# A written order for Sinkhorn-sorted attention and a gated MLP: whole K copies, an early flag, one more turn by DMA, and two output tiles of their own

## The chip, the cores and the metric

One core of one Trainium2 chip runs the kernel. The core has five instruction queues: PE (TensorE, the matrix products), DVE (VectorE), ACT (ScalarE), POOL (GpSimd) and SP (SyncE, which here only issues DMAs). Each runs its own list of instructions in order and waits on semaphores for the others. Sixteen DMA engines, shared by all queues, move data. The metric is device time in microseconds of one execution; smaller is better.

## The reference

The inputs are q, k and v of 4 batches, 8 heads, 768 positions and 64 dimensions, one 8x8 matrix for each head (`sort_net`), and the weights of the second part.

```python
P = sort_net
for _ in range(5):
    P = P - np.max(P, axis=-1, keepdims=True)
    P = np.exp(P)
    P = P / (np.sum(P, axis=-1, keepdims=True) + 1e-09)
    P = P / (np.sum(P, axis=-2, keepdims=True) + 1e-09)
k_sorted = np.einsum('bhij,bhjcd->bhicd', P, k_b).reshape(B, H, S, D)
v_sorted = np.einsum('bhij,bhjcd->bhicd', P, v_b).reshape(B, H, S, D)
# in each of 8 blocks of 96 positions:
attn = softmax(scale * q_b @ k_sorted^T);  x = attn @ v_sorted     # to (4, 768, 512)
...
h = np.maximum(x @ w_in, 0.0)                                      # 512 -> 1024
u, v = h[..., :512], h[..., 512:]
v_n = (v - mean(v)) / np.sqrt(var(v) + 1e-06)
v_s = np.einsum('ts,bsd->btd', w_spatial, v_n) + b_spatial[None, :, None]
return ((u * v_s) @ w_out).astype(np.float32)
```

So each batch goes through mixing K and V by P, attention in blocks, and a gated MLP whose gate mixes the 768 positions by `w_spatial`.

## The kernel before

The whole program is written out as a list of some 350 short items in the string `ORDER`. Each item names a unit (a function `u_XX`) and its arguments, and a loop at the end calls them in that order; each unit adds its instructions to the queues of the engines that it uses. The order of an engine's queue is therefore the order of the items that use it, across units. There is no scheduler behind it. Waits follow from the data and from the buffers.

An item such as `KT:2:DA:0:1` reads: unit KT, PSUM tile `ps2`, copied out half by DVE and half by ACT, batch 0, pair of heads 1. There are four PSUM tiles (`ps0` to `ps3`), and each unit that takes one waits until the copy of its previous user is done. A copy letter is A (ACT), D (DVE), or two letters, which split the copy into halves, side by side. The units that matter here, with the lines that the profile names:

- `L` (L156): a load issued by POOL, converted to bf16 on the way; q, k and v of a batch, the two halves `wv` and `wu` of `w_in`, the halves `wsa` and `wsb` of `w_spatial`, and `wo`. Loads of q, k, v and w_spatial share eight buffers (`ld`).
- `ID`, `MA`, `MB`, `MC`: the identity matrix and the masks made of it. `SK` (L223): one of five rounds that normalise P (L231 to L244), on DVE and ACT. `DM` (L219): products of zeros on PE. `PR` (L249): P spread to 128 partitions. `P0` (L263): batch 0's masked P on DVE, two heads at a time. `PC`: P copied from PSUM to SBUF for POOL. `PD` (L275): the masked P of the other batches on POOL.
- `QT` and `QQ` (L307): Q turned by PE, one or two pairs of heads. `KT` and `VT` (L363): 12 products that mix and turn K or V of a pair of heads. `VB` (L381): V turned back (batch 0). `VM` (L390): V mixed without a turn (other batches), and `VC` (L403): eight DMAs on SP that copy it, four for each half of the blocks, from `vm` to `vb`.
- `SC` (L422 and L427): the scores of a pair of heads and half of the blocks (`ih`), and their exponential on ACT. `AT` (L468, L475, L476): the products with V on PE, the reciprocal and the product with it on DVE, into `x_sb`.
- X must be turned for the MLP. `XT` (L498) does half of one `ih` with eight PE transposes and a copy. `XD` (L486) does a whole `ih` with one DMA transpose, issued on SP. Before, batches 0 and 1 use XT, batches 2 and 3 XD.
- `WT` (L504): w_spatial turned. `VP` (L514): the v half of `x @ w_in`, one or two tiles of 128 positions. `ST`, `LN`, `LA` (L531 to L543): its statistics and normalisation. `UP` (L557): the u half. `SP` (L569, L575): the spatial product and the bias. `GT` (L585): the gate, on DVE or POOL. `OP` (L595): the output product for two tiles of 128 positions, `OE` (L107 on ACT, L109 on DVE) its copy to `o_sb`, `OS` (L610) the DMA that writes it. `o_sb` has two buffers of two tiles each.
- `CK` (L620, L621) tests whether any sum left the range in which the softmax without a maximum is safe, `CF` (L634 to L636) adds the tests to a flag, `LF` (L639) loads the flag into a register of every engine. At the end a branch on it (L696) would run a general path; for these inputs it is not taken.

All copies of one kind share L107 and L109, since `copy` is a helper.

## Time and profile before

| | |
|---|---|
| median of 3 runs | 164.24 us (164.0 to 164.69) |
| the profiled execution's own time | 163.99 us |
| its span, first to last instruction | 162.2 us |
| PE busy | 147.9 us (91%) |
| DVE busy | 117.7 us (73%) |
| ACT busy | 84.3 us (52%) |
| POOL busy | 33.7 us (21%) |
| DMA moved | 23.20 MB |

Times in the text are microseconds from the start of the span. The span is divided into 40 slices of about 4 us; a digit is the busy share of a slice in tenths:

```profile
PE   6988999899999979999999999999999999999700
DVE  4797899667897853748898888789787798267500
ACT  3144999858976476577654453557400155402420
DMA  2999999999999990479985996002059200243370
```

PE is nearly full from the third slice to the 37th; the DMA engines are full until the 15th, which is when the loads of the first three batches and the weights come in. A view by line groups the instructions of one source line and shape; the chain of waits goes back from the last instruction, at each step to what released it.

### The profile page before, as it was taken

How to read it: one execution, taken by the hardware profiler on the slowest of the kernel's cores; microseconds unless marked ns; L12 is line 12 of the kernel's file. 1: busy time of each engine (PE TensorE's matmuls, PEld its weight loads, DVE VectorE, ACT ScalarE, POOL GpSimd, SP SyncE). 2: the span in 40 equal slices, each digit the busy share in tenths (PEclk: the TensorE clock that was granted, in tenths of full speed). 3: DMA queues.
4: the chain of work that ended last, by engine and by line, in shares of the span. 5: the costliest groups of instructions: out<-in, count | busy, mean ns of one | idle time of the engine just before them, and what ended most of it. 6: DMA issues, size and time to landing. Idle time of an engine off the chain costs nothing.

```text
span 162.2 us, 3967 instructions
## 1 busy us (share of the span) xinstructions
PE 147.9 (91%) x1646; PEld 89.5 (55%) x1657; DVE 117.7 (73%) x265; ACT 84.3 (52%) x118; POOL 33.7 (21%) x39
## 2 busy tenths in 40 slices
PE   6988999899999979999999999999999999999700
PEld 2345777756677755455657656555666445655300
DVE  4797899667897853748898888789787798267500
ACT  3144999858976476577654453557400155402420
POOL 7946322470000434280000001600000000120000
PEclk9999999999999999999999999999999999999995
DMA  2999999999999990479985996002059200243370
GB/s 12 191 204 205 203 205 205 210 220 237 271 206 204 206 172 0 69 133 148 184 188 94 225 149 195 0 36 97 0 107 237 113 0 0 91 172 129 129 250 25
DMA packets 27351, 23.20 MB, mean 143 GB/s; under 512 B 7232, under 2 KB 24128, under 8 KB 27328
## 3 DMA queue, kind: packets, MB, share of 16 engines
q0 software_dynamic: 14864, 12.19, 48.5%
q1 hardware_dynamic: 12464, 10.70, 25.8%
q8 instruction: 14, 0.23, 0.5%
q14 instruction: 9, 0.07, 0.1%
HBM read 24.78 MB, written 6.29 MB: 192 GB/s over the span
## 4 chain that ended last, share of the span: by engine, by line
PE 78%; ACT 7%; DVE 6%; DMA 2%; issue 2%; DVEq 0%; ACTq 0%
PE ps L569 20%; PE ps L557 13%; PE ps L514 13%; PE ps L595 11%; PE ps L468 4%; PE ps L422 4%; PE ps L363 3%; PE ps L390 3%; PE ps L307 3%; ACT ex L427 2%; ACT kt L107 2%; PE ps L498 2%; DMA out_dram<-o_sb 1%; PE ps L504 1%; ACT o_sb L107 1%
## 5 line engine op out<-in xcount | busy, mean ns | idle before, releaser
L569 PE MATMUL ps<-wspT,v_sb 128*128 128x384 bf16 x192 | 33.2, 326 | 0.0
L427 ACT ACTIVATE ex<-ps 96x768 bf16<-96x768 f32 x32 | 24.4, 806 | 12.4 <-PE ps L422 12.3
L585 POOL TENSOR_TENSOR gt<-z,u_sb 128x768 bf16<-128x768 f32 x7 | 11.4, 1640 | 92.7 <-DVE z L575 42.1
L569 PEld LDWEIGHTS <-v_sb 128*128 128x128 bf16 x192 | 18.2, 98 | 11.9 <-issue 0.2
L575 DVE TENSOR_TENSOR z<-ps,b_bc 128x768 f32<-128x768 f32 x16 | 15.3, 957 | 11.6 <-PE ps L569 11.5
L557 PE MATMUL ps<-xT,w_in_sb 128*128 128x384 bf16 x128 | 23.3, 326 | 0.0
L476 DVE TENSOR_TENSOR x_sb<-ps,rec_all 96x512 bf16<-96x512 f32 x32 | 22.0, 687 | 1.1
L514 PE MATMUL ps<-w_in_sb,xT 128*128 128x512 bf16 x89 | 22.2, 379 | 0.4
L595 PE MATMUL ps<-w_out_sb,gt 128*128 128x512 bf16 x93 | 22.0, 379 | 0.2
L107 ACT COPY o_sb<-ps 128x1024 f32<-128x1024 f32 (+1 forms) x12 | 9.8, 835 | 14.8 <-PE ps L595 12.9
L531 DVE BATCH_NORM_STATS2 stats<-v_sb 128x6 f32<-128x512 bf16 x24 | 16.2, 677 | 1.0 <-ACT v_sb L113 0.9
L113 ACT ACTIVATE v_sb<-ps 128x1024 bf16<-128x1024 f32 (+1 forms) x8 | 7.4, 920 | 17.6 <-PE ps L514 17.6
L557 PEld LDWEIGHTS <-w_in_sb 128*128 128x128 bf16 x128 | 11.8, 98 | 7.6
L595 PEld LDWEIGHTS <-gt 128*128 128x128 bf16 x96 | 9.2, 98 | 10.2
L514 PEld LDWEIGHTS <-xT 128*128 128x128 bf16 x96 | 9.0, 98 | 9.6 <-DVE x_sb L476 0.2
L113 ACT ACTIVATE u_sb<-ps 128x768 bf16<-128x768 f32 x13 | 10.6, 812 | 5.1 <-PE ps L557 5.0
L107 ACT CAST kt<-ps 128x768 bf16<-128x768 f32 (+1 forms) x14 | 8.7, 641 | 7.9 <-PE ps L363 5.5
L468 PEld LDWEIGHTS <-ex 96*128 96x128 bf16 x256 | 10.5, 97 | 3.6 <-issue 0.3
L468 PE MATMUL ps<-vb,ex 96*128 96x65 bf16 x256 | 11.9, 193 | 0.1
L219 PE MATMUL ps<-warm 128*128 128x512 bf16 x35 | 9.9, 436 | 1.3 <-DVE warm L192 1.3
L422 PE MATMUL ps<-qT,kt 64*128 64x96 bf16 x256 | 9.5, 204 | 1.6 <-ACT kt L107 1.3
L422 PEld LDWEIGHTS <-kt 64*128 64x128 bf16 x256 | 6.2, 94 | 6.9 <-issue 3.8
(87 smaller groups left out, 179.0 us busy)
## 6 DMA issues: line engine op xcount, KB each, us to landing
out_dram<-o_sb SPq DMA_DIRECT2D x9, 512.0 KB, 4.3
q_in<-in_q_dram POOLq DMA_DIRECT2D x4, 768.0 KB, 18.0
k_in<-in_k_dram POOLq DMA_DIRECT2D x4, 768.0 KB, 15.1
v_in<-in_v_dram POOLq DMA_DIRECT2D x4, 768.0 KB, 21.5
vb<-vm SPq DMA_DIRECT2D x24, 99.0 KB, 3.1
out_dram<-o_sb SPq DMA_DIRECT2D x6, 256.0 KB, 3.2
...
```

Of the source, the lines that this page charges most:

```text
L107: nc.scalar.copy(out=out, in_=in_)
L113: nc.scalar.activation(out=out, in_=in_, func=AF.Relu)
L422: nc.tensor.matmul(t[:, hh, 0:HW].rearrange("p (g x) -> p g x", g=G)[:, :, ii * TB:(ii + 1) * TB], lhsT=kT[rows, i * BLK:i * BLK + 128], r ...
L427: nc.scalar.activation(out=e_tile(b, hp, ih).rearrange("p h (x g) -> p h x g", g=G), in_=t[0:BLK, :, 0:HW].rearrange("p h (g x) -> p h x g ...
L468: nc.tensor.matmul(t[:, hh, ii * VW:ii * VW + D + 1], lhsT=e[:, c:c + 128], rhs=vb[b % 2][:, ih * NI + ii, 2 * hp + hh, 0:D + 1], start=Tr ...
L476: nc.vector.tensor_mul(out=x_sb[:, hp].rearrange("p i (h d) -> p h i d", h=2), in0=tv[:, :, :, 0:D], in1=_raw_ap(rec, 0, [rec.ap[0], [NI, ...
L514: nc.tensor.matmul(t[:, x, :], lhsT=st["xT", b][:, n // 3, kc, (n % 3) * 128:(n % 3 + 1) * 128], rhs=w_in_sb[:, kc, DH:DFF], start=(kc == ...
L531: nc.vector.bn_stats(out=stats, in_=st["v_sb", b, n])
L557: nc.tensor.matmul(t[:, x, 0:HW], lhsT=w_in_sb[:, kc, mc * 128:(mc + 1) * 128], rhs=st["xT", b][:, ih, kc, :], start=(kc == 0), stop=(kc = ...
L569: nc.tensor.matmul(t[:, x, 0:HW], lhsT=st["v_sb", b, n][:, mc * 128:(mc + 1) * 128], rhs=wspT[:, 3 * x:3 * x + 3, n, :], start=(n == 0), s ...
L575: nc.vector.tensor_add(out=z.rearrange("p (x c) -> p x c", x=2), in0=t[:, :, 0:HW], in1=b_bc.rearrange("p (x c) -> p x c", x=2),)
L595: nc.tensor.matmul(t[:, x, :], lhsT=st["gt", b, mc][:, (n0 + x) * 128:(n0 + x + 1) * 128], rhs=w_out_sb[:, mc, :], start=(mc == 0), stop=( ...
```

## The change

The change rewrites `ORDER` and adds three units. The new order does the following, beside many moves of single items:

- K is copied out of PSUM whole, by ACT (9 times) or DVE (7 times). Before, 7 of 16 copies were split.
- `PC` stands behind the four `P0`, and the six `DM` between `PR` and the first `KT` are gone. There are 18 products of zeros instead of 36. All four Q pairs of batch 0 are turned ahead of P. The identity is made behind the first load, and the masks earlier.
- The loads come in the order q0 k0 v0 v1 q1 k1 wsa wv wu v2 wsb k2 q2 k3 v3 wo q3 (before: q0 k0 v0 v1 k1 q1 wv wsb wu wsa q2 k2 v2 wo v3 k3 q3).
- X of batch 1 is turned by `XD` instead of `XT`.
- `CK`, `CF` and `LF` stand in the middle of the last batch's MLP instead of at the end.
- The last batch's output tiles 4 and 5 are single tiles: `OH` (products), `OI` (copy, into a buffer of the kind that `z` uses), `OJ` (DMA). Tiles 0 to 3 stay in pairs.

The diff, whole:

```diff
@@ -16,35 +16,35 @@
 
 
 ORDER = """
-S0 CO SK:0 L:q:0:0:8 L:k:0:0:8 L:v:0:0:8 L:v:1:0:8 BH SK:1 SK:2 L:k:1:0:8 ID IV:2 MC IV:0 DM:1:6:512 L:q:1:0:8 SK:3
-L:wv MA DM:3:6:512 DM:1:6:512 DM:2:6:512 SK:4 L:wsb QT:1:A:0:0 MB QT:0:D:0:1 QT:3:A:0:2 DM:2:6:512 PR:3 DM:2:6:512
-P0:0:2 KT:1:A:0:0 P0:6:8 L:wu P0:4:6 PC:D P0:2:4 PD:1:0:4 QT:0:D:0:3 L:wsa IV:1 PD:1:4:8 KT:2:DA:0:1 KT:3:DA:0:3
-SC:1:0:0:0 SC:0:0:1:1 KT:2:D:0:2 SC:3:0:0:1 L:q:2:0:8 VT:1:D:0:0 SC:0:0:2:0 L:k:2:0:8 VT:2:D:0:1 SC:3:0:3:1 VB:1:D:0:0
-VT:0:A:0:2 VB:2:D:0:1 VT:3:A:0:3 AT:1:0:0:1 VB:0:A:0:2 L:v:2:0:8 AT:2:0:0:0 L:wo VB:3:D:0:3 PD:3:0:4 SC:1:0:3:0
-AT:0:0:1:1 SC:2:0:1:0 SC:3:0:2:1 AT:1:0:3:1 VM:2:A:1:0 AT:0:0:1:0 VM:3:A:1:1 AT:1:0:2:1 VM:2:A:1:2 XT:0:D:0:1:0
-KT:3:A:1:2 AT:1:0:2:0 KT:0:A:1:0 AT:2:0:3:0 XT:3:A:0:1:2 KT:0:A:1:3 QQ:1:D:1:0 VM:2:A:1:3 XT:0:D:0:0:2 XT:3:D:0:0:0
-SC:1:1:0:0 QQ:2:D:1:2 VC:1:0:4 KT:0:A:1:1 VP:1:D:0:0:1 SC:3:1:2:1 ST:0:0 SC:0:1:3:1 VP:2:A:0:4:5 WT:3:A:5 WT:1:D:4
-VP:0:A:0:3 ST:0:5 PD:2:0:4 SC:2:1:1:0 ST:0:3 SC:1:1:2:0 UP:3:A:0:1:0 VP:2:A:0:2 VC:1:4:8 ST:0:1 ST:0:4 AT:0:1:0:0
-ST:0:2 WT:1:A:3 SC:3:1:3:0 LN:0:0:6 UP:2:A:0:0:1 AT:0:1:2:0 AT:1:1:3:0 LA:0:0 PD:2:4:8 UP:3:A:0:1:1 WT:0:D:0 LA:0:2
-LA:0:1 LA:0:4 AT:2:1:2:1 LA:0:3 XT:1:A:1:0:2 LA:0:5 L:v:3:0:8 WT:3:A:1 UP:0:A:0:0:0 WT:3:D:2 BI SC:1:1:0:1 QQ:2:A:2:2
-AT:3:1:1:0 AT:0:1:3:1 SP:1:0:3 SC:2:1:1:1 XT:0:D:1:1:2 XT:3:A:1:0:0 AT:1:1:0:1 AT:2:1:1:1 SP:0:0:2 XT:2:A:1:1:0
-GT:P:0:3 KT:1:AD:2:3 KT:3:AD:2:2 KT:0:DA:2:0 KT:2:A:2:1 GT:P:0:2 QQ:1:A:2:0 SC:0:2:3:0 VM:3:D:2:3 SP:2:0:1 VM:1:A:2:2
-VM:0:A:2:1 VP:3:D:1:0:1 VM:2:A:2:0 SP:1:0:0 SC:0:2:2:1 SC:2:2:1:1 GT:P:0:1 VC:2:4:8 VC:2:0:4 ST:1:1 VP:3:A:1:4:5
-SC:1:2:1:0 SC:0:2:3:1 GT:P:0:0 UP:2:A:1:0:0 PD:3:4:8 ST:1:0 ST:1:4 VP:3:D:1:2:3 VM:2:A:3:3 VM:1:A:3:0 OP:0:0:2 ST:1:2
-OE:A:0:2 L:k:3:0:8 AT:1:2:3:1 VM:2:A:3:2 UP:3:A:1:1:0 ST:1:5 AT:0:2:2:1 ST:1:3 VM:2:D:3:1 L:q:3:0:8 UP:1:A:1:0:1
-AT:3:2:1:1 LN:1:0:6 UP:0:A:1:1:1 LA:1:1 AT:1:2:3:0 OP:2:0:0 LA:1:0 SC:1:2:0:1 SC:0:2:2:0 OP:3:0:4 LA:1:5 OS:0:2
-OE:D:0:0 LA:1:3 LA:1:4 LA:1:2 AT:2:2:0:1 AT:0:2:2:0 SP:1:1:0 OE:A:0:4 XD:2:1 SC:2:2:0:0 KT:0:DA:3:2 QQ:3:D:3:2
-KT:1:D:3:1 KT:2:AD:3:0 SP:0:1:2 KT:2:A:3:3 OS:0:4 GT:D:1:0 QQ:1:A:3:0 AT:3:2:1:0 AT:0:2:0:0 VP:2:D:2:4:5 VC:3:0:4
-VC:3:4:8 SC:3:3:3:0 SC:1:3:3:1 ST:2:4 XD:2:0 SP:0:1:1 SC:2:3:2:1 GT:D:1:2 SC:1:3:1:1 SP:3:1:3 AT:0:3:3:0 GT:P:1:3
-AT:2:3:3:1 VP:1:A:2:2:3 ST:2:5 VP:0:A:2:0:1 OS:0:0 AT:1:3:2:1 GT:P:1:1 ST:2:3 UP:2:D:2:0:1 OP:1:1:2 SC:3:3:0:0
-OE:D:1:2 ST:2:2 SC:2:3:1:0 UP:0:A:2:1:0 SC:1:3:0:1 ST:2:1 ST:2:0 LN:2:0:6 SC:3:3:2:0 UP:2:D:2:0:0 AT:0:3:1:1 LA:2:5
-LA:2:4 LA:2:2 OS:1:2 UP:1:A:2:1:1 OP:2:1:0 AT:1:3:0:0 OE:A:1:0 LA:2:0 LA:2:3 LA:2:1 OP:3:1:4 AT:2:3:1:0 AT:0:3:2:0
-SP:1:2:1 XD:3:0 AT:2:3:0:1 XD:3:1 GT:D:2:1 OE:A:1:4 SP:0:2:0 SP:1:2:3 GT:D:2:0 SP:0:2:2 OS:1:4 UP:3:D:3:0:0 OS:1:0
-VP:0:D:3:2:3 GT:D:2:2 VP:1:A:3:0:1 ST:3:3 GT:D:2:3 ST:3:2 UP:3:A:3:0:1 VP:0:A:3:4:5 ST:3:1 OP:3:2:2 ST:3:0 OP:2:2:0
-ST:3:5 ST:3:4 OE:A:2:2 LN:3:0:6 UP:1:A:3:1:1 LA:3:1 UP:0:A:3:1:0 LA:3:5 LA:3:3 LA:3:0 LA:3:2 OE:A:2:0 LA:3:4 SP:1:3:2
-SP:3:3:0 GT:P:3:2 SP:0:3:1 OP:2:2:4 GT:D:3:1 OS:2:0 OS:2:2 OE:A:2:4 GT:D:3:0 SP:3:3:3 OP:1:3:0:0:3 GT:D:3:3
-OP:0:3:4:0:3 OP:-1:3:0:3:4 OE:A:3:0:1:2 OP:3:3:2:0:3 CK OS:2:4 OP:-1:3:2:3:4 OE:D:3:2:1:2 OE:A:3:0:0:1 OP:-1:3:4:3:4
-OS:3:0:1:2 OS:3:0:0:1 OE:A:3:2:0:1 OS:3:2:0:1 OS:3:2:1:2 OE:A:3:4:0:1 OS:3:4:0:1 OE:A:3:4:1:2 OS:3:4:1:2 CF:2 LF
+S0 CO SK:0 L:q:0:0:8 ID L:k:0:0:8 BH L:v:0:0:8 L:v:1:0:8 L:q:1:0:8 MA SK:1 IV:0 MC SK:2 L:k:1:0:8 DM:3:4:512
+DM:2:2:512 L:wsa SK:3 L:wv DM:0:2:512 MB SK:4 DM:3:5:512 QT:0:D:0:0 QT:3:A:0:1 QT:1:A:0:2 L:wu DM:2:3:512 DM:3:2:512
+QT:2:A:0:3 PR:3 P0:2:4 P0:0:2 L:v:2:0:8 IV:2 P0:6:8 P0:4:6 PC:D PD:1:0:4 KT:1:A:0:0 KT:2:D:0:1 IV:1 KT:3:D:0:3
+SC:1:0:0:0 L:wsb SC:0:0:1:0 PD:1:4:8 KT:2:D:0:2 L:k:2:0:8 SC:1:0:3:0 VT:3:A:0:0 VT:0:D:0:1 SC:2:0:0:1 SC:1:0:2:1
+VB:3:D:0:0 VB:0:D:0:1 VT:2:A:0:3 AT:3:0:0:0 VT:1:A:0:2 AT:0:0:0:1 SC:2:0:3:1 L:q:2:0:8 VB:3:A:0:3 AT:1:0:1:0 PD:2:4:8
+PD:2:0:4 VM:0:D:1:3 VM:2:A:1:1 SC:3:0:2:0 VB:1:D:0:2 VM:2:A:1:0 AT:0:0:3:0 VM:3:A:1:2 AT:1:0:2:0 QQ:2:A:1:2 AT:0:0:2:1
+QQ:3:D:1:0 SC:1:0:1:1 XT:0:A:0:0:2 AT:2:0:3:1 XT:1:A:0:0:0 AT:3:0:1:1 KT:0:A:1:2 KT:2:D:1:3 KT:3:A:1:0 KT:1:D:1:1
+SC:2:1:2:0 XT:0:D:0:1:0 XT:3:D:0:1:2 SC:1:1:1:0 WT:2:D:1 WT:0:D:2 WT:3:A:0 SC:2:1:0:1 VP:1:A:0:0:1 PD:3:0:4 SC:2:1:3:0
+SC:3:1:2:1 VP:0:A:0:4:5 ST:0:1 VC:1:0:4 ST:0:0 AT:2:1:1:0 VC:1:4:8 VP:1:A:0:2 VP:3:A:0:3 ST:0:5 AT:0:1:2:0 AT:1:1:3:0
+ST:0:3 SC:2:1:1:1 ST:0:4 UP:3:A:0:0:0 ST:0:2 SC:0:1:3:1 UP:2:A:0:0:1 LN:0:0:6 VM:1:A:2:2 AT:0:1:1:1 LA:0:5
+UP:3:A:0:1:1 LA:0:3 LA:0:1 AT:0:1:0:1 VM:2:A:2:3 LA:0:0 UP:1:A:0:1:0 WT:2:D:5 LA:0:2 VM:0:A:2:0 LA:0:4 WT:3:D:3
+SC:2:1:0:0 VM:1:D:2:1 WT:0:A:4 AT:2:1:2:1 KT:3:A:2:3 KT:1:D:2:2 KT:0:D:2:1 AT:2:1:3:1 BI XD:1:1 SP:3:0:2 AT:0:1:0:0
+XD:1:0 VC:2:4:8 SP:1:0:3 GT:D:0:2 QQ:3:A:2:0 VC:2:0:4 QQ:0:D:2:2 KT:1:A:2:0 SP:2:0:0 SC:0:2:2:1 PD:3:4:8 SC:1:2:0:1
+VP:3:D:1:4:5 L:k:3:0:8 ST:1:4 L:v:3:0:8 SC:2:2:1:1 GT:P:0:3 SC:0:2:3:1 VP:1:A:1:0:1 AT:3:2:2:1 AT:2:2:1:1 L:wo
+SP:0:0:1 GT:P:0:1 KT:2:A:3:2 VM:3:A:3:3 ST:1:0 VM:1:A:3:1 GT:P:0:0 AT:0:2:0:1 VP:2:A:1:2:3 AT:0:2:3:1 UP:1:D:1:1:0
+SC:3:2:3:0 SC:0:2:2:0 OP:2:0:2 ST:1:1 OE:A:0:2 ST:1:5 AT:3:2:2:0 XD:2:1 VM:0:A:3:2 ST:1:2 UP:1:D:1:0:0 AT:2:2:3:0
+ST:1:3 OP:3:0:0 SC:0:2:0:0 SC:2:2:1:0 OS:0:2 OE:D:0:0 OP:1:0:4 LN:1:0:6 AT:0:2:0:0 LA:1:3 OE:A:0:4 AT:3:2:1:0
+UP:2:A:1:0:1 LA:1:2 LA:1:4 VM:1:A:3:0 XD:2:0 VP:0:A:2:4:5 LA:1:0 KT:1:A:3:0 L:q:3:0:8 LA:1:1 VC:3:0:4 QQ:3:D:3:2
+KT:2:A:3:3 QQ:0:D:3:0 KT:1:A:3:1 ST:2:4 LA:1:5 SC:3:3:2:0 UP:2:D:1:1:1 VC:3:4:8 SC:1:3:0:0 ST:2:5 SC:0:3:1:0
+VP:3:A:2:0:1 AT:0:3:2:0 SC:2:3:3:1 SP:1:1:2 SC:3:3:2:1 SC:0:3:3:0 ST:2:1 VP:2:A:2:2:3 GT:P:1:2 ST:2:0 AT:1:3:3:0
+AT:3:3:1:0 ST:2:2 SP:0:1:1 GT:D:1:1 AT:2:3:0:0 SP:1:1:3 OS:0:0 SP:3:1:0 SC:2:3:0:1 GT:D:1:3 SC:1:3:1:1 UP:0:A:2:1:1
+AT:2:3:0:1 ST:2:3 LN:2:0:6 GT:P:1:0 UP:3:A:2:1:0 XD:3:0 AT:0:3:1:1 AT:2:3:3:1 OP:1:1:4 LA:2:2 OS:0:4 AT:3:3:2:1
+OE:A:1:4 CK UP:0:A:3:0:0 LA:2:3 LA:2:5 LA:2:0 UP:2:A:2:0:1 LA:2:4 UP:1:A:3:1:0 XD:3:1 VP:2:D:3:0:1 LA:2:1 UP:3:D:2:0:0
+VP:1:A:3:4:5 ST:3:0 VP:2:A:3:2:3 OS:1:4 ST:3:1 CF:1 UP:3:D:3:0:1 ST:3:3 ST:3:5 LF OP:2:1:0 UP:0:A:3:1:1 ST:3:2 ST:3:4
+SP:1:2:1 OE:A:1:0 LN:3:0:6 SP:0:2:3 GT:P:2:3 LA:3:0 LA:3:3 GT:D:2:1 OP:1:1:2 LA:3:4 OS:1:0 LA:3:2 SP:2:2:2 OE:A:1:2
+LA:3:1 LA:3:5 GT:P:2:2 SP:1:2:0 GT:P:2:0 SP:3:3:0 GT:D:3:0 SP:1:3:2 OP:3:2:2 OS:1:2 OP:1:2:4 OE:A:2:4 OE:D:2:2
+SP:2:3:1 OP:1:2:0 GT:D:3:1 GT:D:3:2 OS:2:4 OE:A:2:0 SP:0:3:3 OP:2:3:0:0:3 OH:0:3:5:0:3 GT:D:3:3 OH:1:3:4:0:3
+OP:-1:3:0:3:4 OH:-1:3:5:3:4 OH:-1:3:4:3:4 OS:2:2 OP:3:3:2:0:3 OI:D:3:4 OE:A:3:0:1:2 OE:A:3:0:0:1 OS:2:0 OS:3:0:1:2
+OI:A:3:5 OJ:3:4 OP:-1:3:2:3:4 OS:3:0:0:1 OJ:3:5 OE:A:3:2:0:1 OS:3:2:0:1 OE:D:3:2:1:2 OS:3:2:1:2
 """
 
 
@@ -613,6 +613,25 @@
         )
 
 
+
+    def u_OH(ps, b, n, lo=0, hi=4):
+        b, n, lo, hi = int(b), int(n), int(lo), int(hi)
+        if lo == 0:
+            st["o1_ps", b, n] = ps_tile(ps)
+        for mc in range(lo, hi):
+            nc.tensor.matmul(
+                st["o1_ps", b, n][:, 0, :], lhsT=st["gt", b, mc][:, n * 128:(n + 1) * 128], rhs=w_out_sb[:, mc, :],
+                start=(mc == 0), stop=(mc == FC - 1),
+            )
+
+    def u_OI(eng, b, n):
+        b, n = int(b), int(n)
+        st["o1", b, n] = moe.tile([128, S], FP32, name="o1_sb", tag="z", bufs=2)
+        copy(eng, st["o1", b, n][:, 0:DM], st["o1_ps", b, n][:, 0, :])
+
+    def u_OJ(b, n):
+        b, n = int(b), int(n)
+        nc.sync.dma_start(out=out[b, n * 128:(n + 1) * 128, :], in_=st["o1", b, n][:, 0:DM])
 
     def u_CK():
         nc.vector.memset(bad, 0.0)
```

## The prediction

> **What bounds the kernel now.** I read the busy time by stage first, then the chain of waits at both ends, then the DMA issues.
>
> ```profile
> core 0: us, PE busy (x) PEld busy (x) DVE busy (x) ACT busy (x) POOL busy (x), PEclk, DMA share, GB/s
> 12.60:33.00 20.40, 18.62 (x416) 14.73 (x415) 16.58 (x34) 16.90 (x24) 7.68 (x9) 1.00 1.29 205
> 33.00:60.00 27.00, 26.02 (x373) 17.67 (x374) 20.58 (x45) 19.39 (x29) 6.32 (x5) 1.00 1.25 221
> 60.00:153.00 93.00, 92.51 (x784) 52.21 (x790) 71.16 (x136) 42.43 (x56) 10.98 (x8) 1.00 0.49 107
> 153.00:162.20 9.20, 0.07 (x1) 0.00 (x0) 0.53 (x3) 1.66 (x3) 0.00 (x0) 0.79 0.43 150
> ```
>
> From 60 to 153 us PE is busy 92.51 of 93.00 us, so in that stage only less PE work helps. Before 60 us PE has holes, and the DMA engines are saturated (the share counts overlapping packets, hence above 1). The last 9.2 us have no PE work. I also priced each step of the written order by its spacing in the chain (12 products of L569 1.95 us, 12 K products 0.46, 8 transposes of L498 0.34, 8 products of L422 0.28, of L468 0.24, of L514 1.73, of L557 1.30, 12 of L307 0.35) and laid these sums beside the start of each step. From the first K product (13.17) to the first u-and-v product (L514, 32.83) there are 16.7 us of work in 19.7, so 3.0 lost. Another 1.7 is lost up to 60 us, 1.3 of it between 55.9 and 59.7, where batch 2's K products wait for copies. After that nothing is lost.
>
> ```profile
> 11.49 0.35 PE ps L249 x8
> 11.84 1.40 PE ps L219 x6
> 13.24 0.46 PE ps L363 x12
> ...
> 150.88 0.46 issue
> 151.34 0.60 ACT o_sb L107
> 151.95 2.21 DMA out_dram<-o_sb
> ...
> 154.32 1.07 ACT o_sb L107 x2
> ```
>
> At the start the first K product stands behind six warm-up products. At the end the last output copies run on ACT, and wait until 154.19 for a transfer, because the third output tile reuses the buffer of the first.
>
> ```profile
> vb<-vm SPq DMA_DIRECT2D x8, 99.0 KB, 7.9
> ```
> ```profile
> vb<-vm SPq DMA_DIRECT2D x8, 99.0 KB, 2.7
> ```
> ```profile
> xT<-x_sb SPq DMA_TRANSPOSE x4, 5.1
> ```
>
> The first row is for 31 to 38 us, the second for 65 to 71: the same copy lands in 2.7 us when the loads are quiet and in 7.9 while they stream. In the trace's DMA records the first byte comes 4.0 us after the issue then, against 1.3 for a transpose in quiet, and the records of the two queues alternate one for one. The four transposes of before (third row) all run in quiet.
>
> **Start, −0.5 us.** The six products of L219 behind P are gone. The first K product then needs P of its heads, which is second on DVE behind the Q copy (11.4 + 0.55 + 0.33 + 0.41 = 12.7), and the first K load, which landed at 12.58: 12.68 against 13.17. That load is issued 0.6 us later, behind the identity; its bytes queue behind Q's until 8.75, which hides it; if it slipped whole, 13.2 and no gain. P's copy for POOL (0.42) now stands behind all four mask products: the first masks on POOL start at 13.7, not 13.4, and are needed by batch 1's V products after 20 us, so nothing.
>
> **PE work, −1.0 us.** Four units of L498 go (4 × 0.34 = 1.36), and one Q turn moves ahead of P (0.35). The flag's product (0.17) and its read come into the PE stream:
>
> ```profile
> L639 PEldq TENSOR_LOAD <-flag x1: 490/490/490, 153.6 to 153.6; - x1
> ```
>
> 0.5 us on PE, as on ACT, DVE and POOL, which have slack there; SP's 0.9 stands between output issues far from the end. If the flag is late on DVE (two statistics of 0.86 stand near it) PE loses up to 1 more; if the read overlaps running products, 0. Whole K copies (ACT 0.80, DVE 0.95, against halves of 0.48 and 0.55 side by side) cost no PE work, but 0.4 more latency each, and they are queued ahead of other DVE work; that matters below. Dropping 18 warm-up products before the K load costs nothing while the clock holds.
>
> **Wait for the v half of w_in, +2.0 us.** Loads land one after the other: 28.74, 31.28, 34.15, 37.36 for the sixth to ninth, about 3.8 us for q, k or v, 2.9 for half of w_spatial, 2.5 for half of w_in. The change puts half of w_spatial ahead of the v half: 28.74 + 2.87 + 2.54 = 34.15 instead of 31.28. In addition batch 1's vb copies have nothing before them on SP and go once the four vm copies are done, which by PE and ACT work is near 26 us instead of 31.28. Loads under these copies took 3.21 for 2.54 and 3.97 for 2.87, so the v half lands between 34.15 and 36.5; I take 35.6. PE reaches the first L514 after 17.9 us of work from 12.68; with 3.5 us lost, like the 3.0 of before, it is there at 34.1. So 5.0 us are lost up to here instead of 3.0: +2.0, between +0.6 and +2.9.
>
> **Middle, −1.3 + 1.3 us.** With X of batch 1 turned by DMA, the hole at 55.9 to 59.7 goes (−1.3): its K copies came behind the turn's copy. In its place stands a new wait. After the last scores product of batch 1's second half (AT:2:1:3:1) PE has 8.5 us of other work up to VP:3:D:1:4:5, which reads the turned X: three L569 groups (5.85), two Q turns (1.36), K (0.46), an AT (0.24), two scores (0.56). But the transpose can't be issued before DVE has finished that AT, behind two whole K copies (2 × 0.95 + 0.86, together 2.8 us after the product). So the transfer has about 5.9 us. In quiet it takes 5.1 and fits. Here k and v of batch 3 are already queued behind q of batch 2 (their issue needs only batch 1's masks and buffers, free by 34 us) and stream until 62 us or later. The late first byte alone gives 4.6 + 2.7 = 7.3, 1.3 us too late; I take that. Bounds: 0, and 5.2 (second rival). Queued behind it on PE are two scores and the other L514 groups; behind it on SP the other half's transpose and batch 2's vb copies, which then come just in time. From 60 us on I keep the loss at nothing; DVE has 13.1 us of work beside 13.8 of PE in the 14 us that follow, so up to 0.5 can go there.
>
> The Trainium skill ("DMA: Bandwidth & Descriptors", Queues, rings and completion order) says that a DMA engine switches between queues at packets, typically 9 to 17 descriptors. The copies of this trace alternate record by record, which speaks against that for copies; for transposes no run here shows it. By that rule the transpose would lose some 0.5 us to the loads, by the copies' rows several.
>
> **End, −2.2 us.** Before, the last product ends at 152.98, the last copy at 155.40, the last issue is at 155.79 and lands at 159.77; 2.4 us of closing follow. After, rows 4 and 5 of the last batch have tiles of their own, no copy waits for a buffer, and only two halves remain behind the last product, one on ACT (0.59) and one on DVE (0.69). So the last issue comes 0.95 us after the last product, not 2.8. The six 256 KB transfers take 0.67 each at the rate of the records (380 KB per us); the last lands 3.6 to 5.3 after the last product instead of 6.8. Gain 1.5 to 3.0 us, taken 2.2.
>
> **Sum.** −0.5 − 1.0 + 2.0 − 1.3 + 1.3 − 2.2 = −1.7 us: span 160.5 instead of 162.2, and 162.3 instead of the profiled execution's 163.99. The median of the runs lies 0.25 higher; I say 162.4.
>
> **The rivals.**
> - *Both waits are hidden.* The v half lands on time (+0.6) and the transpose takes its 5.1 (0): −0.5 − 1.0 + 0.6 − 1.3 − 2.2 = −4.4, 159.8. For it: loads land at 34.15 by plain addition, PE comes at 34.1. Against it: every copy issued while loads streamed took over 7 us.
> - *The transpose alternates with the loads record by record, and the kernel is slower.* It has 1,536 records of 256 bytes, 96 on each engine. A load's record takes 79 ns, so each of the transpose's waits for one; about 750 records of batch 3's v are left when it starts. Issue 55.7, first byte 59.7, these 750 pairs 4.7 us, the rest 1.0, then 2.0 until it lands (as in quiet): 67.4, where PE stands ready at 62.2. Stall 5.2 instead of 1.3: +3.9, 166.3. It decides from a landing 9 us after the issue: there the 1.7 us of the forecast are used up. For it: the copies do so. Against it: no transpose beside a load in this trace.
> - *The clock.* Warm-up products come 427 ns apart until 4.68 and then 208, though the granted clock reads 1.00 throughout:
>
> ```profile
> 4.25 0.15 PEld L219 LDWEIGHTS <-warm 128*128 128x128 bf16 x1 [0.28 <-issue]
> 4.68 3.12 PEld L219 LDWEIGHTS <-warm 128*128 128x128 bf16 x15 [0.28 <-issue]
> ```
>
> With 13 instead of 24 of them ahead of the Q turns, PE is idle from about 5.8 to 8.8, where before it idled 0.5. If that halves the rate again for as long as the first time (3.4 us of products), 1.7 us are lost: 164.1. The Trainium skill ("TensorE: Matmul & The Clock Gate", The HAM clock gate) has the rate fall after an idle window of about 3.4 us; 3.0 us is just short of it.
> - *The change doesn't do what it says:* the flag read early holds all engines while DVE is behind, +1: 163.4.
>
> **Chances.** Forecast 0.42 (161.2 to 163.8 by its own terms), hidden waits 0.22, alternating 0.27, clock 0.06, flag 0.03. What this kernel's measurement can tell from no change is about 0.5%, 0.8 us: below 163.4 is faster, above 165.1 slower. Faster: 0.35 of the forecast, 0.20 of the hidden waits, 0.01 of the flag: 0.56. Slower: 0.26 of the alternating, 0.04 from upper ends of the others and more stalls in the DVE-bound stretch: 0.33 with 0.03 for waits that I haven't named. Same: 0.11. The range goes from the middle of the hidden waits to the upper part of the alternating: 159.6 to 166.8.
>
> **What would show it.** First K product near 12.7; PE waiting for w_in at the first L514 near 34 to 36; PE waiting for xT before the L514 group of batch 1, and the landing time of its transposes (5, 7 or over 9 us); a hole of 0.5 us on PE at the flag; from the last product to the end of the span 7 us instead of 9.2. Transposes over 9 us would make the forecast wrong, and so would a PE that loses time after 65 us.

## The result, and the profile after

The changed kernel takes 169.68 us (168.37 to 170.46) against 164.22: a ratio of 1.032, interval 1.024 to 1.040. It is slower by 5.5 us where 1.8 us faster was forecast, and lies outside the forecast range. Its profiled execution took 170.46 us, with a span of 168.7. (Ratios here and below leave out executions more than 1.5% above the fastest of their kernel; medians count them, and the profiled execution of experiment 1, at 171.42 us, is one of them.) Two views of the changed kernel's, the slices and the stages:

```profile
PE   6577999879999985799993999999999999899930
PEld 2154778745667652455551655656644555445410
DVE  4886899936989872386974285999965879966430
ACT  3144999959797063446445577226614312013130
POOL 7935427260000070036000001204000013600000
PEclk9969999999999999999998799999999999999997
DMA  2999999999999999801995770025440033006372
```
```profile
core 0: us, PE busy (x) PEld busy (x) DVE busy (x) ACT busy (x) POOL busy (x), PEclk, DMA share, GB/s
13.50:36.00 22.50, 19.52 (x446) 15.83 (x442) 19.81 (x36) 19.65 (x26) 11.45 (x14) 1.00 1.27 213
36.00:61.00 25.00, 24.58 (x311) 15.82 (x313) 20.30 (x43) 16.27 (x23) 1.91 (x2) 1.00 1.27 216
61.00:97.00 36.00, 29.35 (x328) 16.64 (x330) 20.26 (x42) 17.51 (x24) 5.63 (x5) 0.95 0.80 135
97.00:161.30 64.30, 63.44 (x457) 35.06 (x459) 49.55 (x92) 23.12 (x32) 8.88 (x5) 1.00 0.27 85
161.30:168.70 7.40, 0.57 (x3) 0.07 (x1) 0.69 (x1) 0.59 (x2) 0.00 (x0) 0.85 0.57 211
```

The third stage is the news. From 61 to 97 us PE is busy for 29.35 of 36.00 us, in a part of the program where before it was full (92.51 of 93.00 from 60 on). The digits 5 and 7 in the PE row at 63 to 71, and the 3 at 88, are two holes, and behind the second the granted clock falls to 0.8 and 0.7. The end behaves: 7.3 us from the last product to the end of the span, 9.2 before. What PE waited for in this stage, for the second hole what ACT waited for, and the DMA issues of 55 to 75 us:

```profile
engine line waited for: us in total, times, longest us
PE ps L514 <- DMA xT<-x_sb: 3.3, 2, 2.3
PE ps L390 <- ACT o_sb L107: 2.5, 1, 2.5
PE ps L468 <- DMA vb<-vm: 0.4, 1, 0.4
```
```profile
ACT o_sb L107 <- DMA out_dram<-o_sb: 3.2, 1, 3.2
```
```profile
vb<-vm SPq DMA_DIRECT2D x8, 99.0 KB, 4.6
w_out_sb<-in_moe_w_out_dram POOLq DMA_DIRECT2D x1, 512.0 KB, 6.7
xT<-x_sb SPq DMA_TRANSPOSE x2, 8.2
```

- *First hole.* Batch 1's transposes were issued at 56.34 and 60.04 and landed at 64.67 and 68.07: 8.3 and 8.0 us, where the same transfer took 5.1 before, in quiet. Both L514 groups of batch 1 stand in front of them.
- *Second hole, not forecast.* The load of q of batch 3 is now issued at 77.69 (71.41 before) and streams until 88.96. Batch 2's first transpose (issued 77.92) takes 10.1 us beside it. The first output (issued 81.55) lies behind the transpose and lands at 89.75. Until then ACT can't copy the third output tile, because `o_sb` has two buffers. The V products L390 queue behind that copy's PSUM, and start at 90.89, 2.5 us after PE stood ready. After this idling the next L514 group takes 3.47 us instead of 1.73.

I laid the priced steps of the written order beside their starts, as for the prediction. PE's lost time, against the forecast:

| | forecast | measured |
|---|---|---|
| first K product | 12.68 | 14.79 |
| first L514 | 35.6 | 36.21 |
| lost from there to 61 us (1.7 before) | 0.4 | 0.75 |
| lost 61 to 77 (0.1 before) | 1.3 | 4.2 |
| lost 77 to 97 (0.2 before) | 0 | 4.2 |
| lost from 97 to the last product | 0 | 0.6 |
| last product to the end | 7.0 | 7.3 |

The first line is part of the second; the other deviations add up to 9.0 us, and the span is 8.2 over its forecast of 160.5. About 0.5 of the difference of 0.8 is the flag's read, which the prediction counts as PE's work and which stands in the lost time here.

### The profile page after: what moved, and what is told of

Its sections match the earlier page's. It is cut to its first block, busy times and chain, and to the rows that moved or that the text cites. A ratio compares the mean times of both kernels' runs of the same rounds, so it can differ in the third digit from the quotient of the medians.

```text
span 168.7 us, 3850 instructions
## 1 busy us (share of the span) xinstructions
PE 146.8 (87%) x1594; PEld 87.8 (52%) x1607; DVE 119.4 (71%) x260; ACT 81.2 (48%) x111; POOL 36.8 (22%) x40
## 5 line engine op out<-in xcount | busy, mean ns | idle before, releaser
L585 POOL TENSOR_TENSOR gt<-z,u_sb 128x768 bf16<-128x768 f32 x8 | 14.3, 1796 | 94.8 <-DVE z L575 94.8
L569 PE MATMUL ps<-wspT,v_sb 128*128 128x384 bf16 x192 | 33.4, 326 | 0.5 <-DVE z L575 0.4
L514 PE MATMUL ps<-w_in_sb,xT 128*128 128x512 bf16 x89 | 23.4, 397 | 4.8 <-DMA xT<-x_sb 3.3
L569 PEld LDWEIGHTS <-v_sb 128*128 128x128 bf16 x192 | 18.1, 98 | 13.0 <-DVE v_sb L543 0.7
L595 PE MATMUL ps<-w_out_sb,gt 128*128 128x512 bf16 x83 | 20.4, 379 | 0.3
L514 PEld LDWEIGHTS <-xT 128*128 128x128 bf16 x96 | 9.1, 100 | 14.7 <-DMA xT<-x_sb 3.4
L113 ACT ACTIVATE v_sb<-ps 128x1024 bf16<-128x1024 f32 (+1 forms) x11 | 10.4, 946 | 12.2 <-PE ps L514 12.1
L468 PEld LDWEIGHTS <-ex 96*128 96x128 bf16 x256 | 11.1, 97 | 4.9 <-issue 0.9
L468 PE MATMUL ps<-vb,ex 96*128 96x65 bf16 x256 | 12.7, 193 | 0.6 <-DMA vb<-vm 0.4
L595 PEld LDWEIGHTS <-gt 128*128 128x128 bf16 x88 | 8.3, 98 | 9.1
L113 ACT ACTIVATE u_sb<-ps 128x768 bf16<-128x768 f32 x11 | 8.9, 810 | 6.0 <-PE ps L557 5.9
L543 DVE TENSOR_SCALAR v_sb<-v_sb,mv,rstd 128x512 bf16<-128x512 bf16 x24 | 11.3, 511 | 0.0
L475 DVE RECIPROCAL rec_all<-ps 96x8 f32<-96x8 f32 x32 | 6.3, 196 | 5.5 <-PE ps L468 5.1
L307 PE MATMUL ps<-ident,q_in 128*64 128x128 bf16 x192 | 7.3, 231 | 2.5 <-DMA q_in<-in_q_dram 2.5
```

The source lines that it names most:

```text
L113: nc.scalar.activation(out=out, in_=in_, func=AF.Relu)
L468: nc.tensor.matmul(t[:, hh, ii * VW:ii * VW + D + 1], lhsT=e[:, c:c + 128], rhs=vb[b % 2][:, ih * NI + ii, 2 * hp + hh, 0:D + 1], start=Tr ...
L514: nc.tensor.matmul(t[:, x, :], lhsT=st["xT", b][:, n // 3, kc, (n % 3) * 128:(n % 3 + 1) * 128], rhs=w_in_sb[:, kc, DH:DFF], start=(kc == ...
L543: nc.vector.tensor_scalar(out=st["v_sb", b, n], in0=st["v_sb", b, n], scalar1=mv[:, n, 0:1], scalar2=rs[:, n:n + 1], op0=ALU.subtract, op1 ...
L569: nc.tensor.matmul(t[:, x, 0:HW], lhsT=st["v_sb", b, n][:, mc * 128:(mc + 1) * 128], rhs=wspT[:, 3 * x:3 * x + 3, n, :], start=(n == 0), s ...
L585: eng.tensor_mul(out=gt, in0=st["z", b, mc], in1=st["u", b, mc // 2][:, mc % 2])
```

## The experiments

Each ratio is against runs of the kernel before on the same chip. "After" is the changed kernel. Diffs are of the written order, with one item moved or replaced where the minus and plus lines say so.

**1. Load of q earlier** (after):

```diff
-KT:1:A:3:0 L:q:3:0:8 LA:1:1
+KT:1:A:3:0 LA:1:1
-AT:2:2:1:1 L:wo
+AT:2:2:1:1 L:wo L:q:3:0:8
```

> The changed kernel with the load of q of batch 3 moved ahead in POOL's queue, behind w_out, so that it is issued near 62 us instead of 77.7. Theory 'shared DMA engines': the transpose of batch 2's second half (77.9 to 88.1 us in the changed kernel) and the output transfer behind it on the same queue were slow because that load streamed beside them; without it the transpose lands in about 4 us, the output in 3 to 4, the copy that waited for the output's buffer does not wait, PE has no hole at 88 to 91 and no slow products after it: 3.5 to 4.4 us less than the changed kernel, about 165.5. Rival 'buffers': the copy waits for its buffer because there are two of them, whatever else runs: less than 1 us. The load now shares with batch 2's vb copies: up to 1 us is given back at 68 to 72.

Measured: 169.2 us, ratio 1.031 (1.0293 to 1.0327). The second hole went as the theory says: batch 2's transpose now took 3.8 us, and PE is busy 19.84 of 20.00 us from 77 to 97 (17.22 in the changed kernel). But most of the loss came back ahead of it. PE's waits from 60 to 97 us, and the issues of 55 to 75:

```profile
PE ps L514 <- DMA xT<-x_sb: 6.4, 2, 3.5
PE ps L468 <- DMA vb<-vm: 1.0, 2, 0.6
```
```profile
vb<-vm SPq DMA_DIRECT2D x8, 99.0 KB, 10.0
q_in<-in_q_dram POOLq DMA_DIRECT2D x1, 768.0 KB, 17.9
w_out_sb<-in_moe_w_out_dram POOLq DMA_DIRECT2D x1, 512.0 KB, 11.1
xT<-x_sb SPq DMA_TRANSPOSE x2, 10.7
```

Everything in flight at 60 to 72 us got slower at once, with q among it: w_out took 11.1 us instead of 6.7, the vb copies 10.0 instead of 4.6. These sizes are those of the execution of 171.42 us; the other four took 168.8 to 169.2. The cause of the second hole is shown (and again in experiment 10); moving the load here merely chose which hole pays.

**2. X of batch 1 by PE again** (after): `XD:1:1` and `XD:1:0` replaced by four XT units, the first pair behind `GT:D:0:2`, the second behind `KT:1:A:2:0`.

> The changed kernel with X of batch 1 turned by PE again (four units of L498 in place of the two transposes). 'Shared DMA engines': the holes of 62 to 71 us (4.2 us beyond what was lost before 62) go, 1.4 us of PE work comes back: 2.8 us less than the changed kernel, about 166.9. Rival 'DVE and K copies': the holes come from late DVE work, and the four copies that the turns add make them no smaller: within 1 us of the changed kernel.

Measured: 167.4, ratio 1.0154 (1.0129 to 1.018). The wait for xT is gone and 2.2 us are lost there in place of 4.2, in small waits around the extra copies; by the medians it takes 2.3 us less than the changed kernel, by the ratios 2.7, with 1.4 us more PE work in it. The theory had 2.8.

**3. Warm-up kept** (after), 24 products ahead of the Q turns instead of 13:

```diff
-DM:3:5:512 QT:0:D:0:0
+DM:3:5:512 DM:2:6:512 DM:0:5:512 QT:0:D:0:0
```

> The changed kernel with 11 more products of zeros ahead of the Q turns, 24 as in the kernel before. Both theories: products stay 208 ns apart, the first K product comes near 12.8 us instead of 14.8. 'Absorbed': PE then waits for the v half of w_in, which lands at 36.2 whatever the clock does, so the end moves by less than 0.5 us (169.2 to 169.7). Rival 'the clock costs its whole delay': 2.0 us less, 167.7.

Measured: 169.65, ratio 1.0327 (1.0273 to 1.038). PE's start in three kernels (start, duration, line, tile, count, and in brackets the idle time before and what ended it), first before, then after, then this one:

```profile
8.79 1.20 PE L307 MATMUL ps<-ident,q_in 128*64 128x128 bf16 x36 [0.50 <-DMA q_in<-in_q_dram]
```
```profile
9.14 1.82 PE L307 MATMUL ps<-ident,q_in 128*64 128x128 bf16 x36 [2.52 <-DMA q_in<-in_q_dram]
...
14.82 1.38 PE L363 MATMUL ps<-pd,k_in 128*64 128x128 bf16 x34 [0.93 <-DVE pd L263]
```
```profile
8.92 1.20 PE L307 MATMUL ps<-ident,q_in 128*64 128x128 bf16 x36
...
13.12 1.43 PE L363 MATMUL ps<-pd,k_in 128*64 128x128 bf16 x36 [0.94 <-DVE pd L263]
...
36.54 0.61 PE L514 MATMUL ps<-w_in_sb,xT 128*128 128x512 bf16 x1 [2.40 <-DMA w_in_sb<-in_moe_w_in_dram]
37.36 1.91 PE L514 MATMUL ps<-w_in_sb,xT 128*128 128x512 bf16 x4 [0.22 <-issue]
```

The clock rival did happen in the changed kernel: after 2.52 us of idling the Q turns took 1.82 us instead of 1.20. With the warm-up kept they took 1.20 and the first K product came 1.7 us earlier, but the v half of w_in still landed at 36.5, so PE only waited longer for it (2.40 us, where the changed kernel waited 0.96). The first L514 starts at 36.54 instead of 36.21: the wait for w_in swallows the whole start. That the total is the same too is partly chance. PE went to half rate after that wait, and is 1.9 us behind at the next L569 (55.97 against 54.06). It wins this back because the transposes, issued 1.9 us later, landed in 6.1 and 5.3 us and no product waited for them (PE waited 3.0 us for the vb copies instead), and because the 2.51 us of idling before 92.25 were not followed by half rate, as the same 2.51 us were in the changed kernel.

**4. The new end alone** (the kernel before, with the single output tiles and the early flag; `CK` behind `OS:1:0`, `CF:1` behind `ST:3:0`, `LF` behind `UP:1:A:3:1:1`).

> The kernel before with two parts of the change alone: the last batch's output tiles 4 and 5 as tiles of their own, and the flag tested and read in the middle of the last batch. By the tail of the changed kernel (7.3 us from the last product to the end of the span, 9.2 before) and a hole of at most 0.5 us at the flag: 1.4 to 1.9 us less than the kernel before, about 162.5. Rival 'flag holds the engines': the tests (1.75 us on DVE) and the read delay the statistics of the last batch, and the gain is under 0.5 us.

Measured: 162.5 (162.25 to 162.62), ratio 0.9903 (0.9884 to 0.9922). As expected, and faster than either kernel.

**5. Batch 1 by DMA alone** (the kernel before):

```diff
-... AT:3:1:1:0 AT:0:1:3:1 ... AT:2:1:1:1 SP:0:0:2 XT:2:A:1:1:0
+... AT:3:1:1:0 XD:1:0 AT:0:1:3:1 ... AT:2:1:1:1 XD:1:1 SP:0:0:2
```

The three other XT units of batch 1 are left out.

> The kernel before, with one part of the change alone: X of batch 1 turned by two DMA transposes (issued on SP right behind the last AT of each half) instead of four units of L498. Theory (a transpose beside loads takes 8 to 12 us, but costs only what exceeds the time until its reader): the two are issued near 50.5 and 54.5 and land near 59 and 65; their readers on PE would stand near 61 and 65.7, so at most a few tenths are waited, PE has 1.36 us less work: 163.0 to 163.8. Rival (the harm lies in what the transposes take from the loads of v of batch 3 and w_out and from the vb copies of batch 2, whatever their own readers do): 164.5 or more, with PE or ACT waiting for a load or a copy between 60 and 80. The prediction's own middle part would have given 162.9.

Measured: 167.64 (167.19 to 169.49), ratio 1.026 (1.019 to 1.032): slower by 3.7 us. That is in the time range of the rival (164.5 or more), but not by its mechanism: PE's longest wait is for the transposes. The issues of 50 to 56 us, and PE's waits of 50 to 70:

```profile
q0 software_dynamic: 1402, 1.17, 121.9%
q1 hardware_dynamic: 186, 0.05, 5.9%
xT<-x_sb SPq DMA_TRANSPOSE x2, 12.1
```
```profile
PE ps L514 <- DMA xT<-x_sb: 2.4, 1, 2.4
PE ps L468 <- DVE z L575: 0.8, 1, 0.8
PE ps L422 <- ACT kt L107: 0.5, 1, 0.5
PE ps L363 <- DVE z L575: 0.3, 1, 0.3
```

The first transpose, issued at 50.77, landed after 13.7 us, the second after 10.5, and SP itself spent 3.9 and 7.2 us on issuing them (1.5 in quiet). In these 6 us the transposes (second row) moved 0.05 MB and the loads (first row) 1.17. My theory had 8 to 12 us and lacked the issue; the reader's window of 10 us was too short. Not all of the loss is this wait: the two rows with `z`, which the kernel before doesn't have, are waits for PSUM tiles behind DVE, where the products of the turn stood before, so part of the saved work only left holes. This one part of the change is costly in the old order too.

**6. Fewer warm-ups alone** (the kernel before, 13 ahead of the Q turns).

> The kernel before with 13 instead of 24 products of zeros ahead of the Q turns, all else as before. Theory (an idle PE of 2.5 us or more halves its rate, and what that costs is seen only where no later wait swallows it): PE idles from 6.5 to 8.8, the Q turns and P run at half rate, the first K product starts near 14.5 instead of 13.2; the v half of w_in lands at 31.3 as before, and PE, which reached it at 32.8, has no wait there that could swallow the 1.3 us: 165.3 to 165.8. Rival (swallowed by the loads of K, V and q of batch 1 all the same): 164.0 to 164.4, the first L514 still at 32.8.

Measured: 164.79, ratio 1.0052 (1.0035 to 1.0069). It lies between theory and rival. The theory missed because q landed at 8.69, so PE idled only 1.68 us, and the Q turns kept their 1.20.

```profile
8.69 1.20 PE L307 MATMUL ps<-ident,q_in 128*64 128x128 bf16 x36 [1.68 <-DMA q_in<-in_q_dram]
```

The profiled execution took 164.32 and lost nothing at the start (first K product at 13.16, before at 13.17); where the others, of 164.71 to 164.98, lost their time is open.

**7. w_in first, and warm** (after): `L:wv` ahead of `L:wsa`, the turns `WT:2:D:1 WT:0:D:2 WT:3:A:0` behind `UP:1:A:0:1:0`, and the warm-ups of experiment 3.

> The changed kernel with the v half of w_in loaded ahead of the first half of w_spatial (whose three turns go behind the first u products), and with 24 products of zeros ahead of the Q turns. Theory (the late w_in swallowed the cold clock, so only both together pay): w_in lands near 33.5, PE is there near 34, so 2 to 2.5 us less are lost up to the first L514; the transposes of batch 1 are issued as much earlier, into the same loads, and give up to 1 of it back: 167 to 168.2. Rival (the loads, which end at the same time, set the end of the batch-1 waits whatever comes ahead): those waits end near 68 again, 169.3 to 170.

Measured: 171.58, ratio 1.044 (1.038 to 1.050). The rival holds as to the mechanism; its time (169.3 to 170) was 1.6 too low. The v half no longer decides the first L514, which starts at 33.60 instead of 36.21, but the transposes of batch 1 end at the same time (its L514 group starts at 64.73, in the changed kernel at 64.94), and PE, which idled 2.61 us for them, now does that group at half rate. The u products that start at 76.73 in the changed kernel start at 77.79. What the front gains is lost at the next thing that hangs on the same stream of loads.

**8. All four remedies** (after): experiments 1, 2 and 7 together.

> The changed kernel with all four remedies: the v half of w_in first, 24 products of zeros, X of batch 1 by PE, q of batch 3 loaded right behind w_out. Theory (these waits are the whole difference): -2.3 for w_in and the clock, -2.2 for batch 1, -3.0 to -4.0 for the transposes of batch 2 and the output that streamed beside the load of q: 160.5 to 162.5. Rival (the new order costs something by itself, in its PSUM tiles and copies): 164 or more, with the rest lost in many small waits.

Measured: 165.22, ratio 1.007 (1.005 to 1.009), in the rival's range. Between 61 and 97 us PE now loses 1.1 us instead of 8.5: with X of batch 1 on PE and q loaded early, the transposes' waits and the hole of the output are gone together. The rest is as the rival has it: 8.7 us are lost in all against 4.9 before, in pieces of about 1 us (0.9 waiting for v of batch 2 at 44, 0.9 at the first L514, 1.1 behind the copies of the turned X at 60, 0.5 near 141).

**9. k and v of batch 3 behind the transposes** (after):

```diff
-VP:3:D:1:4:5 L:k:3:0:8 ST:1:4 L:v:3:0:8 SC:2:2:1:1 GT:P:0:3
+VP:3:D:1:4:5 ST:1:4 SC:2:2:1:1 GT:P:0:3 L:k:3:0:8 L:v:3:0:8
```

> The changed kernel with the loads of k and v of batch 3 issued behind the first gate product of batch 0 on POOL (near 61.7 instead of 34.6), so that batch 1's two transposes, issued near 56.3 and 58, find no load in flight (those ahead end near 54.7). Theory (the transposes are late because they share the DMA engines with those two loads, record for record): they land in 4 to 5 us, near 60.5 and 63, the waits at 62 to 71 shrink from 4.2 to 0 to 1.2 (the vb copies of batch 2 then share with the loads), and the late hole near 90 stays: 165.5 to 167. Rival (the transposes are slow for another reason, their own issue on SP or DVE's late x): 169 or more, landing still over 7 us.

Measured: 169.45, ratio 1.030 (1.025 to 1.035). The theory's mechanism came true, its time did not. The issues from 55.5 to 60 us and from 60 to 68, and PE from 62 to 76:

```profile
xT<-x_sb SPq DMA_TRANSPOSE x2, 4.3
```
```profile
vb<-vm SPq DMA_DIRECT2D x8, 99.0 KB, 7.8
```
```profile
62.54 1.67 PE L514 MATMUL ps<-w_in_sb,xT 128*128 128x512 bf16 x7 [0.16 <-issue]
...
64.59 1.90 PE L514 MATMUL ps<-w_in_sb,xT 128*128 128x512 bf16 x8
66.33 0.26 PE L468 MATMUL ps<-vb,ex 96*128 96x65 bf16 x3
70.46 0.87 PE L468 MATMUL ps<-vb,ex 96*128 96x65 bf16 x13 [3.88 <-DMA vb<-vm]
71.14 4.03 PE L569 MATMUL ps<-wspT,v_sb 128*128 128x384 bf16 x12
75.11 0.85 PE L363 MATMUL ps<-pd,k_in 128*64 128x128 bf16 x12
```

With no load beside them the transposes take 4.3 us and nobody waits for them: contention with those two loads is shown to be what made them late. But batch 2's vb copies, the next DMAs on SP, now meet the loads and take 7.8 us instead of 2.7. PE stands for 3.88 us, and at half rate the twelve products behind (4.03 us for 1.95) cost 2 more.

**10. As 9, with q behind w_out.**

> As f1, and q of batch 3 is loaded right behind w_out, so that the stream ends near 78, before batch 2's first transpose has gone far and before the output. Theory: both holes go (-4.2 and -4.4), the cold start and the wait for w_in stay: 161.5 to 163.5. Rival (the new order loses several us more in small waits, as the kernel with all remedies did): 165 or more.

Measured: 168.56, ratio 1.025 (1.021 to 1.030), 5 us above the theory. The second hole is gone a second time (from 80 to 97 us PE is busy 16.89 of 17.00 us, 14.22 in the changed kernel); the first is that of experiment 9.

```profile
61.00:80.00 19.00, 14.70 (x125) 7.98 (x126) 7.76 (x16) 7.24 (x10) 7.43 (x7) 0.82 1.18 192
80.00:97.00 17.00, 16.89 (x220) 10.28 (x220) 14.15 (x28) 11.82 (x17) 0.00 (x0) 1.00 0.51 105
```

**11. Loads spread out** (after): k of batch 3 as in the changed kernel, w_out too, v and q behind `GT:P:0:1`, and `VM:1:A:3:1` and `VM:3:A:3:3` moved behind the first output product.

> The changed kernel with only k of batch 3 loaded early (it ends near 58.5), w_out as now, and v and q of batch 3 behind the second gate product on POOL (near 71), the V products of batch 3 that need them moved behind the first output product; order of all else as changed. Theory (every small DMA issued beside a load is late, the transposes of batch 1 and then the vb copies of batch 2; with only 2 us of k and 2.5 us of w_out beside them both come in time): transposes land in 5 to 6 us, vb copies by 69, the waits at 62 to 77 shrink from 4.8 to under 1.5; the load of q ends before the output of batch 0 is waited for, so the hole at 88 to 94 goes too: 162 to 164. Rival (something else in the new order holds PE there): 166 or more.

Measured: 174.21, ratio 1.059 (1.056 to 1.062). Again the transposes are in time (4.0 us), and again the vb copies are not: the first, issued 0.9 us ahead of the load of w_out, landed in 3.4 us, the others, beside it, at 67.5 to 72.1. v of batch 3 then came at 85.9, too late for its products. I had expected them by 69: even one load of 0.5 MB beside them was too much.

**12. The old order, batch 1 by DMA, with room** (the kernel before with the new end, experiment 5's transposes, and v of batch 3 loaded behind `GT:P:0:2`).

> The kernel before with the new end (own tiles, early flag), X of batch 1 by two transposes, and v of batch 3 loaded behind the second gate product on POOL (near 58 instead of 35). Theory (a transpose pays where no load streams beside it): the first, issued at 50.8, shares with v of batch 2 and w_out until 58 and lands near 59; the second, issued near 55, lands near 60; readers near 61 and 65.7; 1.36 us of PE work less than the 162.5 of the old order with the new end: 161.0 to 161.6. Rival (the first still holds SP and lands after 61): 162.5 or more.

Measured: 162.91, ratio 0.9926 (0.990 to 0.995). 4.7 us better than experiment 5, of which the new end is 1.7, but no better than 162.5 without these transposes: the first still took 9.9 us and held SP for 3.8, beside v of batch 2 and w_out. Its 1.36 us of saved PE work are lost again in pieces, 1.1 of them in the waits for `z` of experiment 5.

**13. Whole K copies alone** (the kernel before, seven split copies made whole).

> The kernel before with its 7 split K copies made whole (DVE or ACT, the letter that came first, one changed so that neighbours differ), nothing else. Theory (0.4 us more latency each, hidden behind other PE work except near 14.5 and 56 to 59, where K copies are waited for): +0.3 to +1.0, 164.3 to 165.0. Rival (no cost): 163.8 to 164.2.

Measured: 163.26, ratio 0.9959 (0.994 to 0.998): a gain of 0.8, where I expected a loss. DVE's copies from 57 to 59 us, before, then here, and the PE wait behind them:

```profile
57.18 1.49 DVE L109 CAST kt<-ps 128x384 bf16<-128x384 f32 x3 [0.60 <-ACT kt L107]
```
```profile
59.23 0.34 PE L422 MATMUL ps<-qT,kt 64*128 64x96 bf16 x8 [0.58 <-ACT kt L107]
```
```profile
56.56 1.82 DVE L109 CAST kt<-ps 128x768 bf16<-128x768 f32 x2 [0.18 <-PE ps L363]
```
```profile
58.44 0.35 PE L422 MATMUL ps<-qT,kt 64*128 64x96 bf16 x8 [0.26 <-DVE kt L109]
```

A half costs 0.50 on DVE, a whole 0.91; and a split copy needs both engines, so the pair waits for the slower queue. With whole copies, each engine does its own and the scores start 0.8 us earlier, 0.2 of it gained ahead of 55 us. PE's idling in the hole at 55.9 to 59.7, which I put down to the turn of X, falls from 0.87 to 0.26 us with that turn still on PE.

**14 to 16. Which parts add up** (the kernel before, with: the new end and whole K copies; the own tiles with the flag left at the end; the own tiles and whole K copies, flag at the end).

> The kernel before with two parts of the change: the new end (own tiles, early flag; 162.5 measured) and whole K copies (-0.8 measured alone). Theory (the two act in different places, 55 to 60 and behind 150, and add up): 161.5 to 162.0. Rival (the whole copies' gain was the granted clock's, not theirs): 162.4 or more.

> The kernel before with the last two output tiles in tiles of their own, and the flag left at the end. Theory (the early flag costs 0.3 on PE and saves its one product, its sums and its wait at the end): within 0.4 of the 162.5 with the early flag. Rival (the prediction's term of 0.67 us of PE work for the early flag holds, and the flag at the end costs nothing): 161.8 to 162.0.

> The kernel before with own tiles for the last two output tiles and whole K copies, the flag left at the end. Theory (the early flag costs 0.3 to 0.5 us and the three parts add up): 161.2 to 161.5, below the 161.7 with the early flag. Rival (the flag's cost of 0.5 was chance): 161.6 to 161.8.

| | us | ratio (interval) |
|---|---|---|
| new end, whole K copies | 161.70 | 0.9837 (0.9815 to 0.9859) |
| own tiles only | 162.02 | 0.9857 (0.9835 to 0.9879) |
| own tiles, whole K copies | 161.01 | 0.9811 (0.9786 to 0.9836) |

The first is as expected, the second is its rival's time (162.0), the third is 0.2 below its range. The parts add up, and in both pairs the kernel without the early flag is faster, by 0.5 and 0.7 us: the early read of the flag costs about what the prediction's row of 0.5 us said. The last one is the fastest of all, 3.0 us ahead of the kernel before.

## Why the prediction was wrong

- *The step that failed first is "the late first byte alone gives 4.6 + 2.7 = 7.3, 1.3 us too late; I take that".* The term was too small by its own rows: with the 5.1 us that the prediction gives for a quiet transfer the sum is 7.8, and 8.5 less 2.8 leaves 5.7 us for it, not 5.9, so it would have been 2.1 too late. The trace has 8.3: the first byte 3.9 us after the issue, as said, then 3.6 for the 1,536 records (2.2 alone, in experiment 9) and 0.75 until it landed. The first stall was 2.1. The second half's transpose, which I priced at nothing, could only be issued at 60.04, since SP spent 3.6 us on issuing the first; it stopped PE for 1.0 more, and the vb copies behind it for another 1.0 (the two groups of L468 from 69.85 on take 1.45 us for 0.48). Its last record is at 65.46, but it landed 2.6 us later, with w_out's load beside it; what held it is open, since two of the four transposes of before also took 2.0 for this.
- *A transpose beside loads does not only start late, it shares.* In the DMA records of the changed kernel, from 81 to 85 us, the transpose of batch 2 starts 169, 182, 189 and 180 records in each us and the load of q 168, 186, 187 and 177: one for one, as the second rival has it. From 60 to 63 us, where v's load ran out, it was 765 to 400 in all. In experiment 9, with no load beside it, a transpose gets 815 to 840 per us. That rival was the nearest to the time (166.3), but partly by luck: it put 5.2 us on the first stall, which was 2.1, and had nothing for the second hole. The rule of the Trainium skill ("DMA: Bandwidth & Descriptors", Queues, rings and completion order) is that an engine switches between queues at packets of some 9 to 17 descriptors. Equal counts would also come from packets of equal length, so they don't test it (and the 0.5 us that the prediction drew from it doesn't follow); but from 81.5 to 84.5 us the order in which the records of the two queues start repeats every 32, which is one record of each queue on each of 16 engines. So the engines switch after every record there. Whether a record of the trace is a descriptor or a whole packet, it does not tell.
- *What hung on it was priced without its queue.* The prediction named batch 2's vb copies behind the transposes on SP as coming "just in time" and stopped there. In experiments 1, 9, 10 and 11 PE waited for a DMA in those 61 to 77 us each time. An estimate from the rows in quiet, one transfer after the other: two transposes of 1,536 records at 830 per us, 3.7; eight vb copies, 0.7 apart, 5.6; k and v of batch 3 at 3.8 each and w_out at 2.5, 10.1. That is 19.4 us, from 54.95 (end of the load ahead) to the first K product of batch 3, which by work alone PE reaches near 69: 14 us. Before, that product came at 87.3 and its K was loaded from 70 on, and there was no transpose among it. The estimate is an upper end: the 0.7 is SP's spacing, and only k must be there by then (v is first read at 73.8, w_out at 78.6). So that the stretch is too full is argued, not shown; shown is that with the transposes in it each order of loads that I tried changed only who was late, and that without them (experiments 2 and 8) PE waits there for none of these transfers.
- *"From 60 us on I keep the loss at nothing" failed by 4.8 us.* That step looked at DVE's share, and not at the queues that the load of q was moved past: it now streams beside batch 2's transpose, whose records take 8.4 us for 2.2, and with the transpose goes the output behind it on SP's queue, the copy that needs the output's buffer, and the V products behind that copy. Experiments 1 and 10 remove it by moving that load alone.
- *The hole at 55.9 to 59.7 goes for another reason.* Whole K copies take away most of it (experiment 13); the prediction credited the turn by DMA, and costed the whole copies at nothing where they gain 0.8.
- *The start failed, without consequence.* The clock rival, given 0.06, came true: PE idled 2.52 us, less than the 3.0 that I called just short, and went to half rate. The first K product came at 14.79 instead of 12.68, 1.7 of it by the clock (experiment 3). The next term swallowed it: PE was to wait for w_in at 35.6, and did until 36.2.
- *Right:* the wait for the v half of w_in, in place and size (+2.0 forecast; 0.6 later than said), the end (9.2 to 7.3 where 7.0 was forecast), and the early flag's cost of about 0.5. (The last addition is a little off: 162.3 and 0.25 are 162.5, not 162.4.)

The harmful parts are thus the turn of batch 1 by DMA in the middle of a full stream (+3.7 alone) and an order that brings q's load into the next transposes (4.2 lost from 77 to 97 us), with batch 3's K forward by 14 us as a likely third; the good ones are the own tiles (-2.2) and the whole K copies (-0.8). What the rest of the new order loses in small waits (experiment 8 is 2.7 us slower than the old order with the same end) was not taken apart further.
